# Weights of both layers: a scaled 16-bit magnitude and its sign in the upper halves of zeroed words, the rest added as an integer

## The chip, the cores and the metric

The kernel runs on one core of one Trainium2 chip. The metric is the device time in microseconds, the median of several runs. One core has five instruction streams that matter here: PE (TensorE, matrix products), DVE (VectorE), ACT (ScalarE), POOL (GpSimd) and SP, whose queue issues most of the loads and stores.

## The reference

The inputs reach the kernel as float64. Three stages follow one another; S is 576, and there are 8 batches of 8 heads with 64 columns each.

```python
# attention by 32 landmarks (means of 18 rows of q and of k)
A = sm(q, k_lm); Bm = sm(q_lm, k_lm); C = sm(q_lm, k)
Z = Bm.T / (norm1(Bm) * norminf(Bm) + 1e-06)
for _ in range(6):
    Z = 2 * Z - Z @ Bm @ Z
x = A @ Z @ C @ v            # 4608 x 512 after the heads are joined
# first layer
a = x @ w1; b = x @ w2       # 512 x 1024 each
x = (a * b @ w3) @ w_out     # 1024 x 1024, 1024 x 512
# second layer
h = x @ w_in                 # 512 x 2048
g = where(h > 0, h, exp(min(h, 0)) - 1)
out = g @ w_out2             # 2048 x 512
```

The weights are w1, w2, w3 and w_out of the first layer, and w_in and w_out of the second. They are loaded as the 64-bit patterns of their float64 values and turned into float32 on the chip.

## The kernel before

The conversion works on tiles of 128 x 512 weights. A tile's load brings 4 KB to each partition, eight bytes a weight. The first layer has 40 tiles: 8 of w_out, 16 of w3 (transposed) and 16 of w1 and w2 together (w12). The second has 32: 16 of w_in and 16 of w_out.

**First layer, `bits_job`.** The upper 32 bits of a weight hold its sign, its 11-bit exponent and 20 bits of the fraction. ACT writes their absolute value as float32 (L120) and the scaled lower 32 bits as an integer (L122). DVE clamps the absolute value (L124), shifts it left by three and masks it (L126), and puts the sign and the exponent's top bit back (L128). POOL then adds the two as integers (L133); for the first two tiles of w3 DVE adds. Two tiles, one from each of the buffer pools `cvp` and `stp`, go as one job of 17 such pairs in `ORDER`; six single tiles of w12 follow. The operations of a pair are written in turn: both L124, both L126, both L128.

**Second layer, `join_bits`.** ACT takes the absolute value of the top 16 bits as bfloat16 (L162) and the next 32 bits, scaled, as float32 (L167). DVE clamps the 16 bits (L169), shifts the exponent into place (L170), puts the sign on (L171) and keeps a copy of sign and exponent alone (L172). POOL multiplies the rest by that copy (L174) and adds the leading part (L176). The results are split into two parts and written to DRAM, from where the second layer reads them as it goes.

**Order.** All instructions are written out by hand, and each engine works through its own in that order. A `Pipe` holds the conversion jobs as generators. Each tick of the pipe takes each live job one step on and starts one more: the load is issued in the first step, ACT and DVE work in the next, POOL adds in the one after. Raw tiles have three buffers in each pool, the others two. Until about 117 us a loop takes a tick, then one or two steps of the first batch's attention; a w3 tile that is done goes at once into the product of w3 and w_out (L630), which PE accumulates over eight tiles. Then the units of the first layer run (products L742 to L744 and L769 to L771), with the remaining w12 tiles, the next batches' attention and the second layer's conversions as `fill` between them. The second layer's units (L847 to L849 and L906 to L908) take the time from some 640 us on.

Of the kernel before, what the change touches and what calls it, by code (L numbers as in the profile page):

```python
# [8 lines left out]
F32 = mybir.dt.float32  # L9
F32R = mybir.dt.float32r  # L10
BF16 = mybir.dt.bfloat16
U16 = mybir.dt.uint16
U32 = mybir.dt.uint32
AF = mybir.ActivationFunctionType
ALU = mybir.AluOpType
# [39 lines left out]
W3B = 5  # L55
AH = 1
LT = 1
M_MIN = 2.0 ** -15
M_MAX = 122879.9921875
E_MIN = 14336.0  # L60
E_MAX = 18416.0


@with_exitstack
def nystrom_moe_kernel(ctx, tc, qT, kT, vm, vr, w12, w3T, w_out1, w_in2, w_out2, out):
    nc = tc.nc
    pe, dve, act, pool, sp = nc.tensor, nc.vector, nc.scalar, nc.gpsimd, nc.sync
# [28 lines left out]
    class Conv:  # L96
# [6 lines left out]
        def t(self, what, tag, dt, bufs=2):  # L103
            return self.p.tile([128, 512], dt, name=f"{self.nm}_{what}", tag=tag, bufs=bufs)

    def bits_job(jobs, ahead=2, late=1):

        n = 512
        for c in jobs:
            c.raw = c.p.tile([128, 2 * n + 2], U32, name=f"{c.nm}_raw", tag="raw", bufs=3)
            sp.dma_start(out=c.raw[:, 0 : 2 * n], in_=c.src.bitcast(U32))
            c.low, c.top = c.raw[:, 0 : 2 * n : 2], c.raw[:, 1 : 2 * n : 2]
        for _ in range(ahead):
            yield
        for c in jobs:
            c.b, c.r = c.t("b", "cx", U32), c.t("r", "ct", U32)
            act.activation(c.b.bitcast(F32), c.top.bitcast(F32), AF.Abs)  # L120
        for c in jobs:
            act.mul(c.r, c.low, 2.0 ** -29)  # L122
        for c in jobs:
            dve.tensor_scalar(c.b.bitcast(F32), c.b.bitcast(F32), M_MIN, M_MAX, op0=ALU.max, op1=ALU.min)  # L124
        for c in jobs:
            dve.tensor_scalar(c.b, c.b, 3, 0x3FFFFFFF, op0=ALU.logical_shift_left, op1=ALU.bitwise_and)  # L126
        for c in jobs:
            dve.scalar_tensor_tensor(c.b, c.top, 0xC0000000, c.b, op0=ALU.bitwise_and, op1=ALU.bitwise_or)  # L128
        yield
        for c in jobs:  # L130
            if callable(c.x):
                c.x = c.x()
            (dve if c.on_dve else pool).tensor_tensor(c.x.bitcast(U32), c.b, c.r, op=ALU.add)  # L133
        for _ in range(late):
            yield
        for c in jobs:
            if c.done is not None:
                c.done()
# [3 lines left out]
    def hold(what):  # L142

        while what in held:
            yield
        held.add(what)

    def join_bits(c, ahead=2, ready=lambda: True):

        n = 512
        c.raw = c.p.tile([128, 4 * n + 4], U16, name=f"{c.nm}_raw", tag="raw", bufs=3)
        sp.dma_start(out=c.raw[:, 1 : 1 + 4 * n], in_=c.src.bitcast(U16))
        c.top = c.raw[:, 4 : 4 + 4 * n : 4]
        c.mid = c.raw.bitcast(U32)[:, 1 : 1 + 2 * n : 2]
        for _ in range(ahead):
            yield
        while not ready():
            yield  # L160
        c.y = c.t("y", "cy", BF16)
        act.activation(c.y, c.top.bitcast(BF16), AF.Abs)  # L162
        yield
        yield from hold("join")
        c.two, c.tt = c.t("s", "cs", U16, 1), c.t("t", "ct", F32)
        c.lead = c.t("p", "cp", U16)
        act.mul(c.tt, c.mid, 2.0 ** -36)  # L167
        yb = c.y.bitcast(U16)
        dve.tensor_scalar(yb, yb, E_MIN, E_MAX, op0=ALU.max, op1=ALU.min)  # L169
        dve.tensor_scalar(c.lead, yb, E_MIN, 8.0, op0=ALU.subtract, op1=ALU.mult)  # L170
        dve.scalar_tensor_tensor(c.lead, c.top, 0x8000, c.lead, op0=ALU.bitwise_and, op1=ALU.bitwise_or)  # L171
        dve.tensor_scalar(c.two, c.lead, 0xFF80, None, op0=ALU.bitwise_and)  # L172
        yield
        pool.tensor_tensor(c.tt, c.tt, c.two.bitcast(BF16), op=ALU.mult)  # L174
        c.x = c.x()
        pool.tensor_tensor(c.x, c.tt, c.lead.bitcast(BF16), op=ALU.add)  # L176
        held.remove("join")
        yield

# [15 lines left out]
    def wo_job(c, dst):  # L195
        yield from join_bits(c)
        yield from first_part(f"{c.nm}_hi", c.x, dst[:, 0, :])
        sp.dma_start(out=dst[:, 1, :], in_=c.x)
# [3 lines left out]
    def wh_first(c, p):  # L202
        def ready():
            if "wx" in held:
                return False
            held.add("wx")
            return True

        def half():
            wx[p] = c.p.tile([128, 7, 256], F32, name=f"wx{p}", tag="wx")  # L210
            return wx[p][:, 0:2, :].rearrange("p a n -> p (a n)")

        c.x = half
        yield from join_bits(c, ready=ready)

    def wh_second(c, p):


        c.x = lambda: wx[p][:, 2:4, :].rearrange("p a n -> p (a n)")
        yield from join_bits(c, ready=lambda: p in wx)  # L220
        x = wx[p]
        a11, a12, a22, a21, s1, s2, s3 = [x[:, k, :] for k in range(7)]
        pool.tensor_tensor(s1, a21, a22, op=ALU.add)
        pool.tensor_tensor(s3, a11, a21, op=ALU.subtract)
        yield
        pool.tensor_tensor(s2, s1, a11, op=ALU.subtract)
        pool.tensor_tensor(a21, a12, s2, op=ALU.subtract)
        for k in range(0, 7, 2):
            m = min(2, 7 - k)
            yield  # L230
            yield from first_part(
                f"wh{p}{k}", x[:, k : k + m, :].rearrange("p a n -> p (a n)"),
                wh_d[p][:, 0, k : k + m, :].rearrange("p a n -> p (a n)"),
            )
        sp.dma_start(out=wh_d[p][:, 1, :, :], in_=x)
        yield
        held.remove("wx")
# [13 lines left out]
    cvp = att_ctx.enter_context(tc.tile_pool(name="cvp", bufs=1, side="right"))  # L251
# [12 lines left out]
    def load_in(b, which):  # L264
        if which == "v":
            t = att.tile([128, 5, DM], F32, name=f"v{b}", tag="v")
            sp.dma_start(out=t[:, 0:4, :], in_=vm[b])
            sp.dma_start(out=t[0:64, 4, :], in_=vr[b])
        else:
            t = att.tile([128, NP, S], F32, name=f"{which}{b}", tag=which)  # L270
            sp.dma_start(out=t, in_=(kT if which == "k" else qT)[b])
        loaded.setdefault(b, {})[which] = t
# [246 lines left out]
    class Landmarks:  # L519
# [7 lines left out]
        t, ps = Attention.t, Attention.ps  # L527
# [86 lines left out]
    stp = start_ctx.enter_context(tc.tile_pool(name="start", bufs=1))  # L614

    with tc.manual_schedule():
# [48 lines left out]
        def w12_next(p, on_dve):  # L665
            return w12_conv(p, *w12_todo.pop(0), on_dve)
# [5 lines left out]
        for o in ORDER:  # L672
            if o == "A":
                k, n_wo = n_wo, n_wo + 1
                wo = Conv(cvp, f"wo{k}", w_out1[k * 128 : (k + 1) * 128, :], False, x=lambda k=k: wo_tile(k))
                pair = [wo, w3_next(stp, k < E2)]
            elif o == "P":
                pair = [w3_next(cvp, False), w3_next(stp, False)]
            elif o == "B":
                pair = [w12_next(cvp, False), w3_next(stp, False)]  # L680
            elif o == "W":
                pair = [w12_next(cvp, False), w12_next(stp, False)]
            pipe.add(bits_job(pair, ahead=AH, late=LT))
        n_late = len(w12_todo)
        while w12_todo:
            pipe.add(bits_job([w12_next(cvp, False)]))

        for w in PRE:
            if w != "-":
                load_in(0, w)  # L690
            pipe.tick()
# [88 lines left out]
        for p in range(NPAIR):  # L780
            pipe2.add(wh_first(Conv(cvp, f"w2{2 * p}", w_in2[2 * p]), p))
            pipe2.add(wh_second(Conv(cvp, f"w2{2 * p + 1}", w_in2[2 * p + 1]), p))
            for f in (2 * p, 2 * p + 1):
                c = Conv(cvp, f"wo2{f}", w_out2[f * 128 : (f + 1) * 128, :])
# [4 lines left out]
        wh, wo2, ys, tv, yb = {}, {}, {}, {}, {}  # L789
# [160 lines left out]
        for u in range(nu + LAG):  # L950
            if u < nu:
                b, n, fc = units[u]
# [48 lines left out]
        for u in range(1, n2 + LAG2):  # L1001
            if u < n2:
                i, p = units2[u]
# [73 lines left out]
```

## Time and profile before

| what | us |
|---|---|
| median of 3 runs | 1425.52 |
| lowest and highest of them | 1424.61 and 1427.34 |
| the profiled execution | 1424.75 |
| its span, first to last instruction | 1423.0 |
| PE busy in the span | 1360.9 |
| DVE busy | 1079.5 |
| ACT busy | 628.9 |
| POOL busy | 369.6 |

The busy times are sums over the whole span. The stages differ: a stage is to be read by its own busy times, and by what the engine that is full in it does. The mean granted clock of PE is 0.989 of its full speed.

### The profile page before, as it was taken

How to read it: one execution, taken by the hardware profiler on the slowest of the kernel's cores; microseconds unless marked ns; L12 is line 12 of the kernel's file. 1: busy time of each engine (PE TensorE's matmuls, PEld its weight loads, DVE VectorE, ACT ScalarE, POOL GpSimd, SP SyncE). 2: the span in 40 equal slices, each digit the busy share in tenths (PEclk: the TensorE clock that was granted, in tenths of full speed). 3: DMA queues.
4: the chain of work that ended last, by engine and by line, in shares of the span. 5: the costliest groups of instructions: out<-in, count | busy, mean ns of one | idle time of the engine just before them, and what ended most of it. 6: DMA issues, size and time to landing. Idle time of an engine off the chain costs nothing.

```text
span 1423.0 us, 27084 instructions
## 1 busy us (share of the span) xinstructions
PE 1360.9 (96%) x10848; PEld 1176.8 (83%) x10848; DVE 1079.5 (76%) x1934; ACT 628.9 (44%) x1263; POOL 369.6 (26%) x379
## 2 busy tenths in 40 slices
PE   5787999999999999999999999999999999999998
PEld 2235788888787889899899899898998999989987
DVE  7988777788677786744887878878787877878774
ACT  5535454444343545333454443534443444444442
POOL 4452336354264363421301101011110101011000
PEclk9988999999999999999999999999999999999999
DMA  8744454573546543253965564655646556555440
GB/s 306 242 148 139 168 177 142 180 264 101 183 154 216 184 136 114 92 219 113 419 245 186 178 244 158 224 196 198 224 156 239 183 190 231 186 205 188 180 160 30
DMA packets 59470, 266.78 MB, mean 187 GB/s; under 512 B 5584, under 2 KB 14800, under 8 KB 47056
## 3 DMA queue, kind: packets, MB, share of 16 engines
q0 software_dynamic: 12672, 140.51, 27.3%
q1 hardware_dynamic: 46672, 124.54, 25.4%
q8 instruction: 85, 1.39, 0.4%
q14 instruction: 41, 0.34, 0.1%
HBM read 223.08 MB, written 41.94 MB: 186 GB/s over the span
## 4 chain that ended last, share of the span: by engine, by line
PE 83%; DVE 10%; DMA 4%; issue 1%; ACT 1%; SPq 0%; POOL 0%; DVEq 0%; ACTq 0%
PE o L908 9%; PE o L907 9%; PE o L906 9%; PE hm L847 8%; PE hm L848 8%; PE hm L849 8%; PE y L769 5%; PE ab L742 4%; PE ab L743 4%; PE ab L744 4%; PE y L771 4%; PE y L770 4%; PE m L322 2%; DVE w_b L128 1%; DVE w_b L124 1%
## 5 line engine op out<-in xcount | busy, mean ns | idle before, releaser
L847 PE MATMUL hm<-yb,wh 128*128 128x256 f32 x1008 | 285.3, 283 | 3.2 <-DVE g L865 1.7
L848 PE MATMUL hm<-yb,wh 128*128 128x256 f32 x1008 | 285.0, 283 | 0.0
L849 PE MATMUL hm<-yb,wh 128*128 128x256 f32 x1008 | 284.9, 283 | 0.0
L908 PE MATMUL o<-wo,el 128*128 128x512 f32 x576 | 225.6, 392 | 0.0
L907 PE MATMUL o<-wo,eh 128*128 128x512 f32 x576 | 225.3, 391 | 0.0
L906 PE MATMUL o<-wo,eh 128*128 128x512 f32 x576 | 224.0, 389 | 0.0
L878 ACT ACTIVATE t<-m 128x512 f32<-128x512 f32 x144 | 89.9, 624 | 300.5 <-DVE m L876 300.5
L793 POOL DMA_DIRECT2D wh<-wh_d x72 | 39.6, 551 | 612.3 <-PE hm L849 605.1
L847 PEld LDWEIGHTS hm<-yb,wh 128*128 128x128 f32 x1008 | 192.9, 191 | 6.7 <-DVE g L865 1.9
L848 PEld LDWEIGHTS hm<-yb,wh 128*128 128x128 f32 x1008 | 192.9, 191 | 2.8
L849 PEld LDWEIGHTS hm<-yb,wh 128*128 128x128 f32 x1008 | 193.0, 191 | 0.0
L769 PE MATMUL y<-gh,w3oh 128*128 128x288 f32 x512 | 159.7, 312 | 2.9 <-DVE w3ol L71 2.9
L742 PE MATMUL ab<-ath,mh 128*128 128x288 f32 x512 | 156.7, 306 | 2.2 <-DVE g L753 2.2
L881 DVE SCALAR_TENSOR_TENSOR t<-m,t 128x512 f32<-128x512 f32 x144 | 99.1, 688 | 77.9 <-ACT m L879 77.9
L743 PE MATMUL ab<-atl,mh 128*128 128x288 f32 x512 | 151.9, 297 | 0.0
L771 PE MATMUL y<-gh,w3ol 128*128 128x288 f32 x512 | 151.5, 296 | 0.0
L770 PE MATMUL y<-gl,w3oh 128*128 128x288 f32 x512 | 151.4, 296 | 0.0
L744 PE MATMUL ab<-ath,ml 128*128 128x288 f32 x512 | 151.3, 295 | 0.0
L769 PEld LDWEIGHTS y<-gh,w3oh 128*128 128x128 f32 x512 | 96.6, 189 | 39.6 <-issue 22.3
L908 PEld LDWEIGHTS o<-wo,el 128*128 128x128 f32 x576 | 108.1, 188 | 22.6
L906 PEld LDWEIGHTS o<-wo,eh 128*128 128x128 f32 x576 | 108.5, 188 | 20.9
L907 PEld LDWEIGHTS o<-wo,eh 128*128 128x128 f32 x576 | 108.1, 188 | 21.2
(148 smaller groups left out, 2710.2 us busy)
## 6 DMA issues: line engine op xcount, KB each, us to landing
wh<-wh_d POOLq DMA_DIRECT2D x72, 1792.0 KB, 7.8
wo_raw<-in_w_out_dram SPq DMA_DIRECT2D x24, 512.0 KB, 5.3
k<-in_kT_dram SPq DMA_DIRECT2D x8, 1152.0 KB, 7.5
q<-in_qT_dram SPq DMA_DIRECT2D x8, 1152.0 KB, 5.1
yd<-ysb SPq DMA_DIRECT2D x16, 576.0 KB, 3.6
yin<-yd SPq DMA_DIRECT2D x9, 1024.0 KB, 9.8
out_dram<-osb SPq DMA_DIRECT2D x36, 256.0 KB, 2.3
w_raw<-in_w3T_dram SPq DMA_DIRECT2D x16, 512.0 KB, 5.2
```

Of the source, the lines that this page charges most:

```text
L742: pe.matmul(p[:, :NH], mh[:, cs], ah[:, blk, :], start=(blk == 0), stop=False)
L743: pe.matmul(p[:, :NH], mh[:, cs], al[:, blk, :], start=False, stop=False)
L744: pe.matmul(p[:, :NH], ml[:, cs], ah[:, blk, :], start=False, stop=(blk == 1))
L769: pe.matmul(a[oc][:, :NH], w3o_hi[fc][:, os_], gh, start=(fc == 0), stop=False)
L770: pe.matmul(a[oc][:, :NH], w3o_hi[fc][:, os_], gl, start=False, stop=False)
L771: pe.matmul(a[oc][:, :NH], w3o_lo[fc][:, os_], gh, start=False, stop=(fc == K1 - 1))
L847: pe.matmul(o, ah, bh[:, kk, :], start=(kk == 0), stop=False)
L848: pe.matmul(o, ah, bl[:, kk, :], start=False, stop=False)
L849: pe.matmul(o, al, bh[:, kk, :], start=False, stop=(kk == 1))
L906: pe.matmul(a, eh[:, ts_], w[:, 0, :], start=first, stop=False)
L907: pe.matmul(a, eh[:, ts_], w[:, 1, :], start=False, stop=False)
L908: pe.matmul(a, el[:, ts_], w[:, 0, :], start=False, stop=last)
```

## The change

Both conversions now work on the top 16 bits. ACT writes their absolute value, scaled by 2^-112, as bfloat16, so that a shift by three bits leaves the exponent where float32 has it. DVE clamps that pattern from above and multiplies it by eight in one instruction, as an integer of 16 bits, and then joins it with the sign, writing to the upper halves of 32-bit words whose lower halves have been zero since the kernel's start. POOL (DVE for two tiles) adds the scaled 32 bits that follow, rounded to an integer. The words are two tiles for each of the two pools, used in turn, and set to zero by four memsets on POOL ahead of the first load. The loads of the first layer's weights go to an address two bytes off, as those of the second layer already did.

```diff
+    zeroed = {}
+    def words(c):
+        ring = zeroed[c.p]
+        ring.append(ring.pop(0))
+        return ring[-1]
+    def make_words(p, nm):
+        zeroed[p] = [p.tile([128, 512], U32, name=f"{nm}{k}", tag=f"{nm}{k}") for k in range(2)]
+        for t in zeroed[p]:
+            pool.memset(t.bitcast(F32), 0.0)
+    def load_raw(c):
+        n = 512
+        c.raw = c.p.tile([128, 4 * n + 4], U16, name=f"{c.nm}_raw", tag="raw", bufs=3)
+        sp.dma_start(out=c.raw[:, 1 : 1 + 4 * n], in_=c.src.bitcast(U16))
+        c.top = c.raw[:, 4 : 4 + 4 * n : 4]
+        c.mid = c.raw.bitcast(U32)[:, 1 : 1 + 2 * n : 2]
+    def high_parts(jobs):
+        for c in jobs:
+            c.m = c.y.bitcast(U16)
+            dve.tensor_scalar(c.m, c.m, H_MAX, 8.0, op0=ALU.min, op1=ALU.mult)
+        for c in jobs:
+            c.b = words(c)
+            dve.scalar_tensor_tensor(
+                c.b.bitcast(U16)[:, 1:1024:2], c.top, 0x8000, c.m, op0=ALU.bitwise_and, op1=ALU.bitwise_or
+            )
     def bits_job(jobs, ahead=2, late=1):
...
-            act.activation(c.b.bitcast(F32), c.top.bitcast(F32), AF.Abs)
+            c.y, c.r = c.t("y", "cy", BF16), c.t("r", "ct", U32)
+            act.activation(c.y, c.top.bitcast(BF16), AF.Abs, scale=2.0 ** -112)
         for c in jobs:
-            act.mul(c.r, c.low, 2.0 ** -29)
-        for c in jobs:
-            dve.tensor_scalar(c.b.bitcast(F32), c.b.bitcast(F32), M_MIN, M_MAX, op0=ALU.max, op1=ALU.min)
-        for c in jobs:
-            dve.tensor_scalar(c.b, c.b, 3, 0x3FFFFFFF, op0=ALU.logical_shift_left, op1=ALU.bitwise_and)
-        for c in jobs:
-            dve.scalar_tensor_tensor(c.b, c.top, 0xC0000000, c.b, op0=ALU.bitwise_and, op1=ALU.bitwise_or)
+            act.mul(c.r, c.mid, 2.0 ** -13)
+        high_parts(jobs)
...
     def join_bits(c, ahead=2, ready=lambda: True):
...
-        c.two, c.tt = c.t("s", "cs", U16, 1), c.t("t", "ct", F32)
-        c.lead = c.t("p", "cp", U16)
-        act.mul(c.tt, c.mid, 2.0 ** -36)
-        yb = c.y.bitcast(U16)
-        dve.tensor_scalar(yb, yb, E_MIN, E_MAX, op0=ALU.max, op1=ALU.min)
-        dve.tensor_scalar(c.lead, yb, E_MIN, 8.0, op0=ALU.subtract, op1=ALU.mult)
-        dve.scalar_tensor_tensor(c.lead, c.top, 0x8000, c.lead, op0=ALU.bitwise_and, op1=ALU.bitwise_or)
-        dve.tensor_scalar(c.two, c.lead, 0xFF80, None, op0=ALU.bitwise_and)
+        c.r = c.t("r", "ct", U32)
+        act.mul(c.r, c.mid, 2.0 ** -13)
+        high_parts([c])
         yield
-        pool.tensor_tensor(c.tt, c.tt, c.two.bitcast(BF16), op=ALU.mult)
         c.x = c.x()
-        pool.tensor_tensor(c.x, c.tt, c.lead.bitcast(BF16), op=ALU.add)
+        pool.tensor_tensor(c.x.bitcast(U32), c.b, c.r, op=ALU.add)
...
+        make_words(cvp, "cw")
+        make_words(stp, "sw")
         for w in PRE:
```

## Rows read from the trace of the kernel before

**Rows 1.** Busy time by stage: stage, its length, each engine's busy us, clock, DMA.

```profile
core 0: us, PE busy (x) PEld busy (x) DVE busy (x) ACT busy (x) POOL busy (x), PEclk, DMA share, GB/s
0.00:18.50 18.50, 7.21 (x12) 3.11 (x13) 10.31 (x18) 8.57 (x13) 5.62 (x11) 1.00 0.91 349
18.50:61.30 42.80, 35.10 (x137) 13.95 (x136) 42.59 (x75) 23.96 (x43) 23.60 (x18) 1.00 0.73 250
61.30:117.00 55.70, 36.70 (x312) 15.23 (x311) 46.00 (x91) 21.82 (x40) 24.44 (x17) 0.79 0.57 189
117.00:150.00 33.00, 26.31 (x236) 21.52 (x236) 27.27 (x63) 19.80 (x45) 6.39 (x5) 0.93 0.38 120
...
200.00:600.00 400.00, 389.58 (x4381) 337.94 (x4380) 298.65 (x619) 183.30 (x438) 189.71 (x183) 1.00 0.49 167
```

**Rows 2.** Costs by line, 0 to 150 us: busy us, mean ns, idle before.

```profile
L124 DVE TENSOR_SCALAR w_b<-w_b 128x512 f32<-128x512 f32 x32 | 19.8, 637 | 5.7 <-ACT w_b L120 5.4
...
L126 DVE TENSOR_SCALAR w_b<-w_b 128x512 uint32<-128x512 uint32 x32 | 14.1, 464 | 0.2
```

**Rows 3.** Order of time on DVE, one pair: start, duration, instruction.

```profile
20.06 1.50 DVE L124 TENSOR_SCALAR wo_b<-wo_b 128x512 f32<-128x512 f32 x1
...
22.89 0.41 DVE L126 TENSOR_SCALAR wo_b<-wo_b 128x512 uint32<-128x512 uint32 x1
...
23.57 0.68 DVE L128 SCALAR_TENSOR_TENSOR wo_b<-wo_raw,wo_b 128x512 uint32<-128x512 uint32 x1
...
28.26 0.68 DVE L128 SCALAR_TENSOR_TENSOR wo_b<-wo_raw,wo_b 128x512 uint32<-128x512 uint32 x1
```

**Rows 4.** Order of time on POOL.

```profile
9.04 1.56 POOL L133 TENSOR_TENSOR wo<-wo_b,wo_r 128x512 uint32<-128x512 uint32 x1 [8.59 <-DVE wo_b L128]
...
17.86 0.79 POOL L694 MEMSET cvbd<- 128x512 f32 x1
19.69 1.58 POOL L133 TENSOR_TENSOR wo<-wo_b,wo_r 128x512 uint32<-128x512 uint32 x1 [1.03 <-DVE wo_b L128]
```

**Rows 5.** Costs by line on DVE, 160 to 600 us.

```profile
L171 DVE SCALAR_TENSOR_TENSOR w_p<-w_raw,w_p 128x512 uint16<-128x512 uint16 x15 | 10.4, 692 | 0.5
...
L170 DVE TENSOR_SCALAR w_p<-w_y 128x512 uint16<-128x512 uint16 x15 | 4.4, 294 | 1.0
```

**Rows 6.** Order of time on DVE, 61 to 117 us.

```profile
76.81 0.29 DVE L608 SCALAR_TENSOR_TENSOR X<-X,n 128x128 f32<-128x128 f32 x1 [0.71 <-PE n L606]
...
83.56 1.46 DVE L441 TENSOR_TENSOR at<-at,asum 128x576 f32<-128x576 f32 x1
...
87.72 2.51 DVE L128 SCALAR_TENSOR_TENSOR w_b<-w_raw,w_b 128x512 uint32<-128x512 uint32 x2
...
104.08 1.24 DVE L388 TENSOR_TENSOR cvbd<-cv,crs 32x128 f32<-32x128 f32 x4 [1.76 <-PE cv L378]
```

**Rows 7.** Order of time on ACT, the conversion's first step of pair 4.

```profile
20.00 0.68 ACT L120 ACTIVATE w_b<-w_raw 128x512 f32<-128x512 f32 x1 [0.57 <-DMA w_raw<-in_w3T_dram]
```

**Rows 8.** All instructions of line 162: shortest, median and longest ns.

```profile
L162 ACT ACTIVATE w_y<-w_raw x16: 657/671/730, 152.8 to 555.0; 128x512 bf16<-128x512 bf16 x16
```

**Rows 9.** Loads of lines 154 and 114, from issue to landing.

```profile
DMA to landing us min/median/max: 3.5/5.2/11.1
...
DMA to landing us min/median/max: 3.4/4.7/10.6
```

**Rows 10.** Order of time on DVE, a single tile.

```profile
121.67 0.42 DVE L124 TENSOR_SCALAR w_b<-w_b 128x512 f32<-128x512 f32 x1
...
122.59 0.69 DVE L128 SCALAR_TENSOR_TENSOR w_b<-w_raw,w_b 128x512 uint32<-128x512 uint32 x1
```

**Rows 11.** Costs by line and shape on POOL, 150 to 620 us.

```profile
L174 POOL TENSOR_TENSOR w_t<-w_t,w_s 128x512 f32<-128x512 f32 x16 | 18.7, 1166 | 117.3 <-DVE w_s L172 110.3 <-DVE X L608 4.2 <-ACT wo_t L167 2.8
```

**Rows 12.** Order of time on PE, up to 117 us.

```profile
31.95 3.70 PE L630 MATMUL w3acc<-wo,w 128*128 128x512 f32 x8 [0.82 <-POOL w L133]
...
81.25 0.42 PE L606 MATMUL n<-X 32*32 32x64 f32 x16
...
98.07 5.11 PE L630 MATMUL w3acc<-wo,w 128*128 128x512 f32 x8
```

More of the change, by code (lines that the diff above doesn't have):

```diff
@@ L57 @@
 LT = 1
[L58 to L61, printed above, removed]
+H_MAX = 4079.0
 @with_exitstack
@@ L104, in t @@
             return self.p.tile([128, 512], dt, name=f"{self.nm}_{what}", tag=tag, bufs=bufs)
+    zeroed = {}
[22 more added lines that the diff above has]
+            )
     def bits_job(jobs, ahead=2, late=1):
-        n = 512
         for c in jobs:
-            c.raw = c.p.tile([128, 2 * n + 2], U32, name=f"{c.nm}_raw", tag="raw", bufs=3)
-            sp.dma_start(out=c.raw[:, 0 : 2 * n], in_=c.src.bitcast(U32))
-            c.low, c.top = c.raw[:, 0 : 2 * n : 2], c.raw[:, 1 : 2 * n : 2]
+            load_raw(c)
         for _ in range(ahead):
@@ L118, in bits_job @@
         for c in jobs:
-            c.b, c.r = c.t("b", "cx", U32), c.t("r", "ct", U32)
-            act.activation(c.b.bitcast(F32), c.top.bitcast(F32), AF.Abs)
+            c.y, c.r = c.t("y", "cy", BF16), c.t("r", "ct", U32)
+            act.activation(c.y, c.top.bitcast(BF16), AF.Abs, scale=2.0 ** -112)
         for c in jobs:
-            act.mul(c.r, c.low, 2.0 ** -29)
-        for c in jobs:
-            dve.tensor_scalar(c.b.bitcast(F32), c.b.bitcast(F32), M_MIN, M_MAX, op0=ALU.max, op1=ALU.min)
-        for c in jobs:
-            dve.tensor_scalar(c.b, c.b, 3, 0x3FFFFFFF, op0=ALU.logical_shift_left, op1=ALU.bitwise_and)
-        for c in jobs:
-            dve.scalar_tensor_tensor(c.b, c.top, 0xC0000000, c.b, op0=ALU.bitwise_and, op1=ALU.bitwise_or)
+            act.mul(c.r, c.mid, 2.0 ** -13)
+        high_parts(jobs)
         yield
@@ L148, in join_bits @@
     def join_bits(c, ahead=2, ready=lambda: True):
[L152 to L156, printed above, removed]
+        load_raw(c)
         for _ in range(ahead):
@@ L161, in join_bits @@
         c.y = c.t("y", "cy", BF16)
-        act.activation(c.y, c.top.bitcast(BF16), AF.Abs)
+        act.activation(c.y, c.top.bitcast(BF16), AF.Abs, scale=2.0 ** -112)
         yield
         yield from hold("join")
-        c.two, c.tt = c.t("s", "cs", U16, 1), c.t("t", "ct", F32)
-        c.lead = c.t("p", "cp", U16)
-        act.mul(c.tt, c.mid, 2.0 ** -36)
-        yb = c.y.bitcast(U16)
-        dve.tensor_scalar(yb, yb, E_MIN, E_MAX, op0=ALU.max, op1=ALU.min)
-        dve.tensor_scalar(c.lead, yb, E_MIN, 8.0, op0=ALU.subtract, op1=ALU.mult)
-        dve.scalar_tensor_tensor(c.lead, c.top, 0x8000, c.lead, op0=ALU.bitwise_and, op1=ALU.bitwise_or)
-        dve.tensor_scalar(c.two, c.lead, 0xFF80, None, op0=ALU.bitwise_and)
+        c.r = c.t("r", "ct", U32)
+        act.mul(c.r, c.mid, 2.0 ** -13)
+        high_parts([c])
         yield
-        pool.tensor_tensor(c.tt, c.tt, c.two.bitcast(BF16), op=ALU.mult)
         c.x = c.x()
-        pool.tensor_tensor(c.x, c.tt, c.lead.bitcast(BF16), op=ALU.add)
+        pool.tensor_tensor(c.x.bitcast(U32), c.b, c.r, op=ALU.add)
         held.remove("join")
```

## The prediction

> **What bounds the kernel now.** I read the busy time by stage first [rows 1]: PE is the engine to fill, and from 200 us on it is full (389.58 us busy of 400 between 200 and 600). Before 150 us it is not. There the full engine is DVE: 42.59 of 42.8 us between 18.5 and 61.3, 46.00 of 55.7 up to 117, and 27.27 of 33 up to 150. The first 18.5 us belong to the DMA engines (share 0.91). So a saving on DVE can be worth time only in the first 150 us; after that it must show as fewer waits of PE, and all the idle time of PE between 200 and 600 is 10.4 us.
>
> What DVE does there I read from the costs by line [rows 2]: the weight tiles, 40 of them before 150 us, each with a clamp (L124), a shift and mask (L126), and the joining of the sign (L128), after which POOL adds the rest (L133). Seventeen pairs of tiles come first (numbered below), then six single tiles. L124 has a mean of 637 ns, though it takes 0.42 when nothing is in its way [rows 10]. The order of time shows why [rows 3, 4]: at 20.06 it takes 1.50 us, and POOL's add runs from 19.69 to 21.27; the second L124 stands as long under POOL's second add. A pair's period is therefore (23.57 to 28.26) 4.69 us: two joins of 0.6 from start to start, the wait for POOL's two adds with the L124s squeezed between and behind them, and then the two L126s, 0.68 us from 22.89 to 23.57, which nothing hides.
>
> The Trainium skill ("SBUF — State Buffer", section Who interferes with whom) says the same of the port: DVE in a two-port mode, or with two SBUF inputs, and a reading GpSimd instruction exclude each other for a whole instruction. The rows above agree. By this rule the new, shorter clamp would be shut out just as the old one is, so it is no argument for a larger gain than the one below.
>
> **The change, part by part.** *Conversions before 150 us.* Of each tile's three DVE instructions two remain. The new clamp with multiply on 16-bit data has a row in the second layer's conversion: L170, the same kind of instruction on the same shape, 294 ns [rows 5]; from start to start I take 0.23, as an L126 of 0.41 costs 0.34 [rows 3]. The new join is L171's kind (692 ns) [rows 5] against L128's 0.68 [rows 3]. What no row shows is its output in every other 16-bit place. Below, I bound it by the 0.6 from start to start of L128, which writes the same words; above, by twice that, 1.2, as in the row at 87.72, where POOL holds two joins up to 2.51 [rows 6]. I take 0.61, as reading at a stride already costs L171 nothing. So a tile that is not held up goes from 0.34 + 0.34 + 0.6 to 0.23 + 0.61: 0.44 saved, 0.88 for a pair. Where both clamps lie under POOL's adds, only the two L126s go and the clamp behind the last add gets 0.1 shorter: 0.7 to 0.78 for a pair. The spread between these is small; I take 0.8.
>
> ACT's work keeps its size: Abs of 32-bit words takes 0.68 [rows 7], Abs of 16-bit ones with 16-bit output 671 ns at the median [rows 8]; the scale is a constant of the instruction, and the second multiplication is the same one with another constant. ACT now waits less, since Abs fills a buffer that the join frees, not POOL's add. POOL's add is unchanged. The load goes to an address two bytes off; loads so placed land in 5.2 us at the median, the others in 4.7 [rows 9]. Three raw buffers let a load start about three pairs ahead (some 12 us), which hides 0.5 us; only in the first 20 us, with the DMA engines full, could it cost, at most 1 us. The four memsets are 4 x 0.79 by the memset of the same shape [rows 4]: 3.2 us on POOL, which has nothing else until its first add at 9.04 [rows 4]; without that cover they would delay the first join by as much.
>
> *Up to 61 us.* In the present order the join of pair 4 starts at 23.57. With the first three pairs 0.8 us shorter each, DVE reaches pair 4 early and waits for its data: ACT's Abs of it starts at 20.00, when the load has landed [rows 7]. Then 0.68 for Abs and 0.25 for the clamp put the join at 20.93: 2.6 us gained. From there to the join of pair 11, the last of this stage, there are seven periods with DVE never idle, each 0.8 shorter: 5.6. PE must follow: its products for a tile of w3 take 3.70 us [rows 12] in a period that falls from 4.7 to about 4.0, and it is idle for 42.8 - 35.1 = 7.7 us of the stage [rows 1], so it is nearly, but not quite, the next bound. Stage total 8.2.
>
> *61 to 117 us.* Six pairs and a single. Here DVE waits 9.7 us in all, and a saving ahead of a wait for PE only lengthens the wait. That is so for the pairs ahead of 76.81 and 104.08 [rows 6] and for the one between them whose follower needs the PE result of 81.25 [rows 12], on which DVE would now wait. The first pair of the stage gains 0.9. The fourth gains more: its joins stand under POOL's subtraction of 87.98 to 89.67 and take 2.51 in place of 1.28 [rows 6]; 0.9 earlier they get through, 2.0 in all, of which the next pair, again under POOL's adds, gives back about 1. A multiply at 83.56 [rows 6] that POOL holds up (1.46 for 0.75) gets 0.7 back, and the single gains 0.4. Total 3.0.
>
> *117 to 150 us.* Five single tiles between the first products. There each instruction waits for the one ahead: from L124's start to the join's are 0.92 us [rows 10] against 0.32 for the new clamp, and the join 0.7 against 0.61: 0.5 a tile. Four stand ahead of results that PE waits for; the fifth is followed by an idle DVE. Total 2.0.
>
> *From 150 us.* The 32 tiles of the second layer lose two DVE instructions (0.6 us) and POOL's two floating-point passes, of which the first takes 1166 ns [rows 11] and the second, on the same shapes, about the same, for one integer add of about 1.3: 32 x 1.0 = 32 us of POOL less. Neither bounds this stage. I count 1.0 for PE's waits, between nothing and half of the 10.4 us.
>
> Sum: 8.2 + 3.0 + 2.0 + 1.0 = 14.2. The profiled execution took 1424.75 us, 1.75 more than its span of 1423.0; what lies outside the span stays. The median of the runs is 1425.52, 0.77 higher, and the forecast goes by it: 1411.3.
>
> **The rivals.** *Another engine takes over early.* For it: PE's products need 3.7 of the new 4.0 us [rows 12], loads are at 0.73 of the DMA engines in that stretch [rows 1], and DVE waits more the shorter it gets. Against: the idle 7.7 us of PE just suffice. If only some 6 of them can be taken before 61 us and the next stages give 0.5, the time is 1419.
>
> *More than counted.* The granted clock was 0.79 from 61 to 117 us [rows 1]; the products there took up to 5.11 in place of 3.70 us [rows 12]. If a denser stage keeps the full clock (3 us), and POOL's shorter work frees half of PE's waits after 150 us (5 us in place of 1), 21 us go: 1404. Against it: PE does no more work per us in the waits that remain.
>
> *The joins move under POOL's adds.* What happens at 87.72 could become the rule once the clamp is short: both joins would then cost 1.2 us more a pair. It decides from 0.8 us more on, where a pair's saving is gone. In all 14 pairs after 18.5 us it is 14 x (1.2 - 0.8) = 5.6 lost: 1431. For it: the page of the skill says that the join, too, is shut out. Against: in the steady order of [rows 3] the joins come behind both adds, which the clamps await. A join slowed by its output at a stride would look the same, and decides at 1.05 us from start to start.
>
> *No change.* DVE's saving is real, but PE's order and the loads swallow it: within 3 us of before. Only a PE that is the true bound in both first stages would do that, and [rows 1] shows it idle for a third of the second.
>
> **How the numbers follow.** Forecast (1406 to 1416) 0.62, more than counted 0.13, another engine 0.16, no change 0.04, joins under the adds or slow 0.05. Leaving out the last two and the far ends of the second and third gives 1403 to 1420. A difference of 0.2%, 2.9 us, is about what a measurement of this kernel can tell: faster 0.91, same 0.04, slower 0.05.
>
> **What would show it.** In the new profile: two DVE instructions for a tile, the clamp near 0.29 and the join near 0.69 us where POOL is idle; the pair's period near 4.0 us between 20 and 40; the first product of the first layer (L742) about 11 us earlier; the stage after 200 us as long as before to within a few us. Wrong would be: joins of over 1 us, or DVE idle by a fifth before 61 us while PE is full.

## The result and the profile after

The changed kernel takes 1403.57 us at the median of 4 runs (1403.01 to 1403.94), the kernel before 1426.43 in the runs beside it: a ratio of 0.9841, 95% interval 0.9824 to 0.9858, or 22.9 us faster. The forecast was 14.2 us less, 1411.3. The profiled execution took 1403.01 us with a span of 1401.2, 21.8 less than the span before.

The busy time by stage follows, with the stages cut at the same places of the program as in [rows 1]: the join of pair 11 now starts at 51.09 (it was 60.06), the first product of the first layer at 105.12 (116.71).

```profile
core 0: us, PE busy (x) PEld busy (x) DVE busy (x) ACT busy (x) POOL busy (x), PEclk, DMA share, GB/s
0.00:18.50 18.50, 8.10 (x14) 3.48 (x15) 8.67 (x14) 8.51 (x13) 8.18 (x16) 1.00 0.91 349
18.50:52.30 33.80, 31.94 (x119) 12.38 (x117) 32.23 (x55) 23.51 (x43) 21.67 (x17) 1.00 0.89 303
52.30:105.10 52.80, 38.67 (x331) 16.06 (x330) 40.48 (x78) 21.55 (x39) 23.04 (x17) 0.82 0.61 208
105.10:138.00 32.90, 26.69 (x243) 21.97 (x237) 24.76 (x58) 19.86 (x45) 6.41 (x5) 0.93 0.37 121
187.90:578.30 390.40, 385.64 (x4381) 336.25 (x4380) 274.12 (x561) 183.38 (x438) 157.01 (x154) 1.00 0.50 171
```

The second stage is 9.0 us shorter, and PE, DVE and the DMA engines are all near full in it: 31.94, 32.23 and 0.89 of 33.8. The third gives 2.9 us (2.6 by the start of the product that ends it, the cuts being rounded); the fourth next to nothing (0.45 by the starts of products). The last one, where 1.0 was counted, is 9.6 us shorter (400.0 to 390.4), with 24.5 us less on DVE and 32.7 less on POOL.

The order of time on DVE shows the pair's period, and two joins that POOL holds up:

```profile
20.89 0.74 DVE L129 SCALAR_TENSOR_TENSOR cw<-wo_raw,wo_y 128x512 uint16<-128x512 uint16 x1
...
22.37 1.12 DVE L126 TENSOR_SCALAR wo_y<-wo_y 128x512 uint16<-128x512 uint16 x1
23.41 1.35 DVE L126 TENSOR_SCALAR w_y<-w_y 128x512 uint16<-128x512 uint16 x1
24.68 0.73 DVE L129 SCALAR_TENSOR_TENSOR cw<-wo_raw,wo_y 128x512 uint16<-128x512 uint16 x1
...
28.45 0.28 DVE L126 TENSOR_SCALAR w_y<-w_y 128x512 uint16<-128x512 uint16 x1
28.65 0.73 DVE L129 SCALAR_TENSOR_TENSOR cw<-wo_raw,wo_y 128x512 uint16<-128x512 uint16 x1
...
81.81 1.80 DVE L129 SCALAR_TENSOR_TENSOR cw<-w_raw,w_y 128x512 uint16<-128x512 uint16 x1
...
98.85 1.84 DVE L129 SCALAR_TENSOR_TENSOR cw<-w_raw,w_y 128x512 uint16<-128x512 uint16 x1
```

Pair 4 joins at 20.89 where 20.93 was forecast, and the clamps of pair 5 still stand under POOL's adds (1.12 and 1.35 in place of 0.28), as in [rows 3]. What was a shift and mask behind them is gone. The period is 3.79 from pair 4 to pair 5 (20.89 to 24.68), where it was 4.69 in [rows 3], and 3.97 to the next pair (24.68 to 28.65), where it was 4.85 (28.26 to 33.11); between those two pairs DVE also makes two reductions. So a pair saves 0.9, where 0.8 was forecast.

The order of time on POOL has the four memsets (two a row), and the adds of pairs 4 and 5. The last two rows are the instructions that ran over the joins of 81.81 and 98.85:

```profile
0.74 0.98 POOL L114 MEMSET cw<- 128x512 f32 x2 [0.29 <-POOLq L1075]
...
8.16 1.54 POOL L152 TENSOR_TENSOR wo<-cw,wo_r 128x512 uint32<-128x512 uint32 x1 [5.51 <-ACT w_r L146]
...
21.77 1.56 POOL L152 TENSOR_TENSOR wo<-cw,wo_r 128x512 uint32<-128x512 uint32 x1 [1.59 <-ACT w_r L146]
23.30 1.31 POOL L152 TENSOR_TENSOR w<-sw,w_r 128x512 uint32<-128x512 uint32 x1
25.56 1.57 POOL L152 TENSOR_TENSOR wo<-cw,wo_r 128x512 uint32<-128x512 uint32 x1 [0.95 <-DVE cw L129]
27.10 1.27 POOL L152 TENSOR_TENSOR w<-sw,w_r 128x512 uint32<-128x512 uint32 x1
...
81.70 1.32 POOL L152 TENSOR_TENSOR w<-sw,w_r 128x512 uint32<-128x512 uint32 x1
...
98.70 1.40 POOL L459 TENSOR_TENSOR atl<-atf,ath 128x576 fp32r<-128x576 f32 x1 [5.65 <-ACT ath L458]
```

The first two memsets end at 1.72, and POOL sits idle for 5.51 us ahead of its first add: the cover was there. The rows also show what the new period is made of. The join of 24.68 ends at 25.41, POOL's two adds run from 25.56 to 28.37, one clamp of 0.28 follows, and the next join starts at 28.65. DVE is busy nearly all the while, but POOL's adds are now the longest part of the chain.

Where the lead arose is read by setting the start of the same PE product in one trace against its start in another. This table does so for the changed kernel and for four of the experiments below; a number is how many us earlier than before that product starts.

| product's start before | changed | second layer only | first layer only | DVE's two put back | POOL's pass put back |
|---|---|---|---|---|---|
| 116.7 | 11.6 | -0.1 | 12.0 | 11.2 | 11.0 |
| 152.0 | 12.0 | -0.1 | 12.4 | 11.6 | 11.3 |
| 339.2 | 12.7 | 0.5 | 12.0 | 11.8 | 10.8 |
| 405.7 | 15.4 | 1.8 | 11.9 | 12.6 | 12.9 |
| 460.1 | 21.3 | 7.7 | 11.4 | 16.3 | 17.9 |
| 651.8 | 21.7 | 8.6 | 10.9 | 16.7 | 17.1 |

The changed kernel gains nearly all of it in two places: 12.0 us before 152, and 8.6 us between 339 and 460. The second place was not in the forecast. Three waits of PE in the kernel before stand there, of which the changed kernel has 0.72 us of the first and nothing of the others:

```profile
390.25 1.95 PE L322 MATMUL m<-w_sb,z 64*32 64x512 f32 x16 [2.16 <-DVE at L419]
...
434.91 0.40 PE L742 MATMUL ab<-ath,mh 128*128 128x288 f32 x1 [0.79 <-DVE g L753]
...
451.36 0.40 PE L742 MATMUL ab<-ath,mh 128*128 128x288 f32 x1 [1.44 <-DVE g L753]
```

How the last of them comes about is seen in the order of time on DVE of the kernel before:

```profile
446.51 0.73 DVE L303 TENSOR_REDUCE ksum<-k 128x32 f32<-128x576 f32 x1
447.17 0.68 DVE L169 TENSOR_SCALAR wo_y<-wo_y 128x512 uint16<-128x512 uint16 x1
447.95 0.70 DVE L170 TENSOR_SCALAR wo_p<-wo_y 128x512 uint16<-128x512 uint16 x1
448.69 0.98 DVE L171 SCALAR_TENSOR_TENSOR wo_p<-wo_raw,wo_p 128x512 uint16<-128x512 uint16 x1
449.77 1.17 DVE L172 TENSOR_SCALAR wo_s<-wo_p 128x512 uint16<-128x512 uint16 x1
450.87 0.44 DVE L753 TENSOR_TENSOR g<-ab,a 128x288 f32<-128x288 f32 x1
```

and of the changed one, at the same place of the program:

```profile
426.69 0.74 DVE L312 TENSOR_REDUCE ksum<-k 128x32 f32<-128x576 f32 x1
427.35 0.69 DVE L126 TENSOR_SCALAR wo_y<-wo_y 128x512 uint16<-128x512 uint16 x1
428.13 1.18 DVE L129 SCALAR_TENSOR_TENSOR cw<-wo_raw,wo_y 128x512 uint16<-128x512 uint16 x1
429.20 0.43 DVE L764 TENSOR_TENSOR g<-ab,a 128x288 f32<-128x288 f32 x1
```

From the reduction to the product g, which PE needs, it was 4.36 us and is 2.51. The 16-bit instructions take 0.68 to 1.17 there in place of 0.29, and the join 0.98 before and 1.18 after in place of 0.69 and 0.73; POOL is busy for most of the stretch. Busy time of the kernel before at this place, in two windows of 6 us (columns as above):

```profile
442.00:448.00 6.00, 5.63 (x55) 3.99 (x55) 5.66 (x13) 1.72 (x4) 4.75 (x6) 1.00 0.89 295
448.00:454.00 6.00, 3.97 (x37) 2.83 (x35) 5.83 (x8) 0.83 (x2) 5.48 (x6) 1.00 0.13 47
```

and of the changed kernel:

```profile
421.00:427.00 6.00, 6.00 (x90) 5.45 (x89) 5.79 (x15) 3.96 (x10) 2.83 (x3) 1.00 0.47 151
427.00:433.00 6.00, 6.00 (x65) 4.48 (x63) 5.84 (x9) 1.46 (x4) 5.78 (x7) 1.00 0.52 192
```

In the second window DVE is full in both, 5.83 and 5.84 of 6; PE had 3.97 and has 6.00. A full DVE alone does not say that PE waits for it; the row of 451.36 does. So a stage whose mean was 298.65 of 400 on DVE [rows 1] holds a stretch in which DVE is the bound.

### The profile page after: what moved, and what is told of

The parts are those of the page before. It is cut to its first block, busy times and chain, and to the rows that moved or that the text cites. A ratio compares the mean times of both kernels' runs of the same rounds, so it can differ in the third digit from the quotient of the medians.

```text
span 1401.2 us, 26871 instructions
## 1 busy us (share of the span) xinstructions
PE 1356.7 (97%) x10848; PEld 1175.1 (84%) x10848; DVE 1031.0 (74%) x1830; ACT 628.3 (45%) x1263; POOL 332.5 (24%) x351
## 4 chain that ended last, share of the span: by engine, by line
PE 72%; DVE 2%; DMA 1%; ACT 0%; issue 0%; SPq 0%; ACTq 0%; DVEq 0%
PE o L919 9%; PE o L918 9%; PE o L917 9%; PE hm L858 9%; PE hm L859 8%; PE hm L860 8%; PE y L780 3%; PE ab L753 3%; PE y L782 2%; PE y L781 2%; PE ab L754 2%; PE ab L755 2%; PE m L331 1%; DMA w_raw<-in_w_in_dram 1%; PE n L615 0%; PE cv L387 0%
## 5 line engine op out<-in xcount | busy, mean ns | idle before, releaser
L764 DVE TENSOR_TENSOR g<-ab,a 128x288 f32<-128x288 f32 x128 | 58.1, 454 | 103.2 <-ACT gh L67 60.5
L917 PEld LDWEIGHTS o<-wo,eh 128*128 128x128 f32 x576 | 108.5, 188 | 20.9
```

What stands on the lines that cost most here:

```text
L917: pe.matmul(a, eh[:, ts_], w[:, 0, :], start=first, stop=False)
```

## The experiments

Each kernel was timed in three rounds beside the kernel before, which stood at 1426.5 to 1427.4 us at the median. Where work is added, it goes to a scratch tile or is written over.

**One layer at a time.** The kernel `e1` has the new `join_bits` and the old `bits_job`; `e2` the reverse, with

```diff
-        c.lead = c.t("p", "cp", U16)
+        c.lead = words(c).bitcast(U16)[:, :512]
```

in the old `join_bits`, for want of room.

> The new conversion for the second layer alone, the old one for the first. The trace of the changed kernel is 12.0 us ahead after 200 us and 21.7 us ahead from 520 us on, so 9.7 us came in the first layer's main stage, where the prediction had 1.0. Theory A: the second layer's conversions did that themselves (fewer instructions of DVE and POOL ahead of what PE waits for). Then this kernel is 9 to 10 us faster than before: 1416 to 1418. Theory B: those 9.7 us are a matter of phase; the earlier start moves the conversions and loads to better places. Then this kernel is as before, 1424 to 1427.

> The new conversion for the first layer alone, the old one (with the zeroed words as its buffers for the leading part) for the second. Theory A: only the 12 us of the start are gained: 1413 to 1416. Theory B: all of it: 1403 to 1406. By the prediction's own stages it would be 13.2 us: 1413.

Measured: 1418.68 us for the second layer alone (ratio 0.9940, 0.9926 to 0.9955) and 1414.39 for the first alone (0.9912, 0.9896 to 0.9929). Against 1426.99 that is 8.3 and 12.6, together 20.9 of the 22.9. Theory A fits, `e1` being 0.7 us above its range, and B does not: the late gain belongs to the second layer's conversions themselves, and comes at the same place without the earlier start (7.7 at 460 in the table). The missing 2.0 us are within what the runs leave uncertain (each ratio to some 0.0015, or 2 us). In the profiled executions there is also a difference of clock: after 150 us the granted clock is at half from 391.1 to 394.5 in the kernel before, twice in `e1` (from 353.8 and from 664.4), once in `e2` (from 379.4) and not at all in the changed kernel.

**DVE or POOL.** In `e3` the second layer's conversion has two more instructions of DVE, in `e4` one more of POOL (1.08 us at the median, where the pass that was removed had a mean of 1.17 to 1.19):

```diff
         dve.tensor_scalar(c.m, c.m, H_MAX, 8.0, op0=ALU.min, op1=ALU.mult)
+        dve.tensor_scalar(c.two, c.m, 0xFF80, None, op0=ALU.bitwise_and)
...
             c.b.bitcast(U16)[:, 1:1024:2], c.top, 0x8000, c.m, op0=ALU.bitwise_and, op1=ALU.bitwise_or
         )
+        dve.tensor_scalar(c.two, c.two, 0xFF80, None, op0=ALU.bitwise_and)
```

```diff
+        pool.tensor_tensor(c.two[:, :416], c.b[:, :416], c.r[:, :416], op=ALU.add)
         c.x = c.x()
```

> The changed kernel with the two instructions that DVE lost in the second layer's conversion put back as work on a scratch tile, one ahead of the join and one behind it; POOL stays relieved. Theory A1: it is DVE's own queue, in which the conversions stand ahead of the product that PE waits for. Then 5 to 9 us come back: 1409 to 1413. Theory A2: it is POOL's pass that held the shared port. Then at most 2 us come back: 1403.5 to 1405.5.

> The changed kernel with an extra integer add on POOL ahead of each add of the second layer's conversion, 416 columns wide, about the time of the pass that was removed (1.05 us); DVE stays relieved. Theory A2 (POOL's hold on the port): 5 to 9 us come back: 1409 to 1413. Theory A1 (DVE's queue): at most 2 us: 1403.5 to 1405.5.

Measured: 1408.77 (1407.90 to 1410.98), 5.2 us back, and 1407.43 (1406.78 to 1408.26), 3.9 us back. Neither theory alone: both engines' work counts, and POOL's acts through DVE too. Between the same two products as in the last row of the table of stages, DVE is busy for 285.5 us in `e3` and 279.9 in `e4`, where the changed kernel has 274.1: the added pass of POOL alone lengthens DVE's work by 5.7. In the profiled execution of `e3`, some 3 us of what came back stand in two stretches at half clock (from 342.7 and from 656.8) that the changed kernel does not have.

The second layer's part of the gain is 1414.39 - 1403.57 = 10.8; the two give 9.1 of it, and the difference is within the runs' uncertainty. The traces do have a step that comes with neither: from the product at 429.9 before to the one at 444.9 the lead grows by 2.0 in the changed kernel, by 2.0 in `e3` and by 1.8 in `e4`. In that stretch DVE waits for a slice of q to be loaded, and PE for the g behind it (the row of 434.91). Before and after:

```profile
433.74 0.75 DVE L303 TENSOR_REDUCE qsum<-slice 128x32 f32<-128x576 f32 x1 [4.49 <-DMA slice<-in_qT_dram]
...
415.60 0.75 DVE L312 TENSOR_REDUCE qsum<-slice 128x32 f32<-128x576 f32 x1 [2.33 <-DMA slice<-in_qT_dram]
```

In `e3` the wait is 2.60, in `e4` 3.46. Why the slice keeps DVE waiting for less time was not tested. The kernel with both was not run.

**The place in DVE's queue.** The theory behind A1 was that the conversions cost because they stand right ahead of the product g. `e7` (on the kernel before) and `v3` (on the changed one) write the odd half-steps' conversions behind it:

```diff
             if pipe.busy():
                 pipe.tick()
+            elif hs % 2:
+                behind.append(hs in CONV)
             else:
                 pipe2.tick(hs in CONV)
...
                 ab_product(u)
+                while behind:
+                    pipe2.tick(behind.pop(0))
```

> The kernel before, with the second layer's conversion steps of each odd half-step written behind the next product; nothing else changed. If the old conversions cost by standing ahead of that product in DVE's queue, most of the main stage's gain comes without the change: 1418 to 1422. If it is the sum of DVE's and POOL's work that counts, at most 2 us: 1424.5 to 1427.

> The changed kernel with the second layer's conversion steps of each odd half-step written behind the product of the next unit (the one that PE waits for) in place of ahead of it; the work is the same. If their place ahead of that product is what cost 5.2 us with DVE's two instructions put back, what is left of it goes: 1 to 3 us gained, 1400.5 to 1402.5. If only the sum of DVE's work counts, no change.

Measured: 1426.92 for `e7`, a ratio of 1.0002 (0.9992 to 1.0011): nothing. `v3` has 1401.75 (1399.69 to 1403.76), which overlaps the changed kernel. The order of time on DVE of `e7`, at the place shown above:

```profile
448.68 0.44 DVE L753 TENSOR_TENSOR g<-ab,a 128x288 f32<-128x288 f32 x1
449.04 0.32 DVE L169 TENSOR_SCALAR wo_y<-wo_y 128x512 uint16<-128x512 uint16 x1
...
452.41 0.45 DVE L71 TENSOR_TENSOR gl<-g,gh 128x288 fp32r<-128x288 f32 x1
```

The product now runs right behind the reduction, but its split, which PE needs too, stands behind the conversion in turn, 3.73 us later (it was 0.37). The place ahead of g alone was not the cost. In this stretch DVE is full, and what was moved delays something else. A place behind the split as well was not tried.

**The start.** `e6` adds two 16-bit instructions of DVE a tile to the first layer's conversions only:

```diff
             dve.tensor_scalar(c.m, c.m, H_MAX, 8.0, op0=ALU.min, op1=ALU.mult)
+        if extra:
+            for c in jobs:
+                c.s = c.t("s", "cs", U16, 1)
+                dve.tensor_scalar(c.s, c.m, 0xFF80, None, op0=ALU.bitwise_and)
+            for c in jobs:
+                dve.tensor_scalar(c.s, c.m, 0xFF80, None, op0=ALU.bitwise_and)
```

> The changed kernel with two more 16-bit instructions of DVE (0.23 us each from start to start) for each of the first layer's 40 tiles, between clamp and join, on a scratch tile: DVE's time for a tile is that of before again, all else stays changed. If the start is bound by DVE, as the prediction has it, the 12 us of the first 150 us go: 1413 to 1416, first product of the first layer again near 115 us. If what helped there is that ACT's first step no longer waits for POOL's add, or something else, at most 4 us go: 1404 to 1408.

Measured: 1419.13 (1418.30 to 1419.66), 15.6 us back. On DVE:

```profile
22.78 0.28 DVE L130 TENSOR_SCALAR wo_s<-wo_y 128x512 uint16<-128x512 uint16 x1
...
23.59 0.73 DVE L135 SCALAR_TENSOR_TENSOR cw<-wo_raw,wo_y 128x512 uint16<-128x512 uint16 x1
...
28.19 0.73 DVE L135 SCALAR_TENSOR_TENSOR cw<-wo_raw,wo_y 128x512 uint16<-128x512 uint16 x1
```

The period is 4.60 (23.59 to 28.19), near the 4.69 of before, and the first product of the first layer starts 0.5 us later than before the change: the whole gain of the start is gone, though loads, ACT and POOL work as in the changed kernel. The start is bound by DVE's work at this place, behind POOL's adds, where nothing hides it. The 3 us beyond 12 stand in two stretches at half clock that the changed kernel's trace does not have; in each of them `e6` falls 1.5 us further behind that kernel (columns as above, the clock third from the end):

```profile
354.20:357.60 3.40, 3.40 (x41) 3.12 (x43) 0.34 (x2) 2.45 (x5) 0.00 (x0) 0.50 0.27 106
664.80:668.20 3.40, 3.40 (x18) 3.40 (x18) 3.13 (x7) 0.49 (x1) 1.32 (x3) 0.50 1.14 413
```

`e9` lengthens POOL's part of the first layer by an add of 128 columns a tile, `e8` does each memset four times:

```diff
+            if not c.on_dve:
+                pool.tensor_tensor(c.x.bitcast(U32)[:, :128], c.b[:, :128], c.r[:, :128], op=ALU.add)
```

```diff
-        for t in zeroed[p]:
+        for t in zeroed[p] * 4:
             pool.memset(t.bitcast(F32), 0.0)
```

> The changed kernel with an extra add of 128 columns (about 0.35 us by the length of the full one) ahead of each add of POOL in the first layer's conversions. If a pair's period of about 4.0 us is set by POOL's two adds, under which the clamps stand, each pair gets up to 0.7 us longer: 4 to 9 us, 1408 to 1413. If DVE's own instructions set it, at most 2: 1403.5 to 1405.5.

> The changed kernel with each of its four memsets done four times (12 more of 0.46 us on POOL, 5.5 us in all). In the changed kernel's trace they end at 2.6 us and POOL's first add is at 8.16, so all are hidden: no change within 1 us, 1402.6 to 1404.6. If the first join waits for them or their writes hold DVE up, 1405 or more.

Measured: `e8` 1403.40, no change: the memsets are hidden. `e9` 1407.18 (1405.06 to 1409.63), 3.6 us back, between the two expectations. In its order of time on DVE:

```profile
23.63 1.81 DVE L129 SCALAR_TENSOR_TENSOR cw<-wo_raw,wo_y 128x512 uint16<-128x512 uint16 x1
...
28.11 1.81 DVE L129 SCALAR_TENSOR_TENSOR cw<-wo_raw,wo_y 128x512 uint16<-128x512 uint16 x1
```

The clamps now slip through between POOL's short and long add and it is the joins that stand under POOL (1.81 for 0.73); the period grows to 4.48. That is the rival of the joins under the adds, brought about by longer adds. (Both 4.48 and its counterpart 3.97 hold two reductions.) At the join of pair 11, 4.5 us are lost (55.62 for 51.09), at the first product only 2.0. So POOL's adds set part of the period, as the chain read above has it, and the waits further on take up some of it.

**Trying for a faster version.** POOL's subtraction in the attention's split goes to DVE. In the changed kernel the join of 98.85 stands under it, and the join of 81.81 under the second add of POOL behind it. The edit is made for the first batch (`v1`), for all (`v2`), and for the first together with the edit of `v3` (`v4`):

```diff
-            pool.tensor_tensor(lo, f, hi.bitcast(F32), op=ALU.subtract)
+            (dve if self.b == 0 else pool).tensor_tensor(lo, f, hi.bitcast(F32), op=ALU.subtract)
```

> The changed kernel with POOL's subtraction of the attention's split (1.4 us, two of them before the first product, each with joins of DVE held up behind it, 1.80 and 1.84 us in place of 0.73) moved to DVE for the first batch (0.75 us each). If the hold-ups cost what they show, 1 to 2 us are gained: 1401.5 to 1402.5; if DVE's longer queue takes them, no change.

> The same for all batches: 16 subtractions of 1.4 us leave POOL and cost DVE 0.75 each. If POOL's hold on the port is the larger part of what is left of PE's waits (3.9 us came back with 33 us of POOL's work put back), 1 to 3 us beyond the first batch alone; if DVE's queue is, the same time or 1 to 2 us slower.

> The changed kernel with both edits that gained: the first batch's split subtraction on DVE (1401.2), the odd conversion steps behind the product (1401.8). They act in different stages, so the gains should add: 1399 to 1400.5.

Measured: `v1` 1401.19 (1400.80 to 1403.09; ratio to before 0.9822, 0.9807 to 0.9836), `v2` 1406.57 (1404.72 to 1406.97), `v4` 1401.31 (1399.99 to 1401.58). On DVE of `v1`, the second subtraction with the join ahead of it:

```profile
97.81 0.74 DVE L129 SCALAR_TENSOR_TENSOR cw<-w_raw,w_y 128x512 uint16<-128x512 uint16 x1
98.44 0.74 DVE L459 TENSOR_TENSOR atl<-atf,ath 128x576 fp32r<-128x576 f32 x1
```

Join and subtraction together take less than the held-up join did, and the first product starts 1.5 us earlier than in the changed kernel. `v1` is 2.4 us faster than the changed kernel at the median, with their ranges touching and the intervals of their ratios overlapping, so the runs alone do not settle it. With the edit of `v3` besides, `v4` is no faster than `v1`. `v2` is 5.4 us slower than `v1`: 14 more subtractions off POOL do not pay for 14 more on DVE.

## Why the prediction was right, and where it was not

- **The forecast as a whole** gave a gain, and its larger part is where it was put: 12.0 us before 152 for the 13.2 forecast. The time itself is 2.4 us below the forecast of 1406 to 1416 and only 0.6 us inside the range, whose lower end came from a rival with a chance of 0.13. That it still lies inside is partly luck: the forecast's own mechanism after 150 us was wrong.
- **What bounds the start** was right. `e6` shows it: with DVE's time a tile restored behind POOL's adds, 12.1 us of lead vanish. `e9` adds that POOL's adds are now in the same chain.
- **Up to 61 us**: 8.2 forecast, 9.0 measured (60.06 to 51.09). The first term was exact (pair 4 at 20.89), the seven periods gave 6.3 in place of 5.6, 0.9 each. PE was just able to follow.
- **61 to 117 us**: 3.0 forecast, 2.6 measured (11.59 at the first product less 9.0). As said there, one pair gave back under POOL's adds (81.81); the single's join under POOL's subtraction (98.85) was not foreseen.
- **117 to 150 us**: 2.0 forecast, 0.45 measured. The mechanism was right: by the product at 133.7 the lead had grown from 11.6 to 13.5. Then 1.5 went to the clock, as the order of time on PE shows:

```profile
119.95 0.33 PE L548 MATMUL bs<-ksum,qpad 128*32 128x32 f32 x16 [2.21 <-DVE ml L419]
...
120.61 0.44 PE L781 MATMUL y<-gl,w3oh 128*128 128x288 f32 x1
...
124.50 0.29 PE L755 MATMUL ab<-ath,ml 128*128 128x288 f32 x1
```

PE, ahead by now, waits 2.21 us where it had waited 1.64, and the twelve products behind the wait run at half the rate (granted clock 0.54 of full from 120.0 to 123.3, so nearly all at 1.2 GHz). Before, the same products ran at full clock (1.00 from 133.5 to 136.8). The length of the wait does not settle it: another wait of the changed kernel is as long, and the clock stays full behind it (1.00 from 340 to 344). The row of before, and that one of after:

```profile
133.44 0.33 PE L539 MATMUL bs<-ksum,qpad 128*32 128x32 f32 x16 [1.64 <-DVE ml L410]
...
340.46 0.65 PE L615 MATMUL n<-X 32*32 32x64 f32 x32 [2.27 <-DVE X L605]
```

What else decides is open.

- **From 150 us** is the step that failed: "I count 1.0 for PE's waits, between nothing and half of the 10.4 us." It gave 9.7. POOL's work removed was sized rightly, 32.7 us for 32; DVE's busy time fell by 24.5 where 0.6 a tile, 19.2, was counted. Wrong was to hold all this hidden because of a mean over 400 us. Before, DVE and POOL are full together from 394 to 400 (5.97 and 5.77 of 6) and from 448 to 454, as shown above, and in the second window PE waits; `e1` shows that the second layer's change gains there by itself, `e3` and `e4` that DVE's two instructions bring 5.2 of it and POOL's pass 3.9. The bound of 5.2 us was wrong too. PE's idle time between the two marks fell by only 5.7 us (10.4 to 4.8); the rest was in PE's busy time, 389.58 to 385.64. Part of that is the clock: a product group at half clock takes longer and counts as busy, as in [rows 12]. Before, the wait of 2.16 us at 390.25 was followed by half clock from 391.1 to 394.5; in the changed kernel the same wait is 0.72 and the clock stays full. The lead grows there from 13.2 to 15.4, the shorter wait giving 1.4 of it.
- **The costs**: clamp 0.28 to 0.29 and join 0.73 to 0.74, where 0.29 and 0.69 were taken; so writing every other 16-bit place costs some 0.04 us, far from the bound of 1.2. The memsets took 0.46 each by their starts, not 0.79.
- **The rivals**: "more than counted" is what happened, by half its argument: POOL's and DVE's relief after 150 us, while the clock from 61 to 117 stayed where it was (0.82 for 0.79). Joins under POOL did occur, at 81.81 under an add and at 98.85 under the subtraction, and in `e9` in most pairs up to 45 us; in the change itself they stayed the exception.

What stays open: why DVE waits less for the slice of q near 434 us, and what beyond the length of PE's waits decides over the clock.

## What to carry to other kernels

Read the busy times of a long stage in short windows before calling an engine hidden: a mean of 0.75 can hold stretches at 0.97, and there removed work counts. Idle time of the engine to be filled is no upper bound either, since its work at half clock counts as busy. Where one engine's instructions stretch beside another's, as DVE's did here beside POOL's, relief of both is worth more than the queue of one suggests; but moving work to the fuller of the two cost more than it freed (`v2`). Moving work behind a product in a full queue gained nothing here (`e7`), since the next instruction that PE needs then waited: see first what else stands behind the new place.

## What the runs showed that was not expected

- A wait of PE of 2.21 us was followed by products at half clock for about 3 us, which cost 1.5 us of a lead already won; a wait of 1.64 us at the same place was not, and neither was one of 2.27 us elsewhere.
- A 16-bit clamp that took 0.29 us alone took 1.12 and 1.35 under POOL's adds, and a 16-bit join 1.80 under an add and 1.84 under a subtraction for 0.73: the fast form is held up as the slow one was.
- With an extra add on POOL (0.44 to 0.92 us), it is no longer the clamps but the joins that wait (1.81 us): which instruction is held up depends on the gaps between POOL's instructions.
